# A retention kernel with two feed-forward layers: every load among the retention tiles waits until at most a megabyte of loads is under way ahead of it

## The chip, the cores and the metric

The kernel runs on one core of a Trainium2 chip. The metric is the device time of one execution in microseconds (us); before the change it is 815.48 us, the median of 3 runs (814.66 to 815.95). Names of engines: TensorE (PE in the rows; PEld is its weight load), VectorE (DVE), ScalarE (ACT), GpSimd (POOL) and SyncE (SP), whose queue issues the transfers that are spoken of here.

## What is computed

Retention over 4 batches, 8 heads, 576 positions and 64 channels per head, and then two feed-forward layers without biases on the 2304 tokens of 512 channels:

```python
scores = scale * np.matmul(q, k.transpose(0, 1, 3, 2))
Dmat = np.where(rel >= 0, gamma[:, None, None] ** rel[None, :, :], 0.0)
ret = scores * Dmat[None, :, :, :]
x = np.matmul(ret, v)                       # then (B, H, S, D) -> tokens x 512
h = x @ w_in;  r = np.maximum(h, 0.0);  x = (r * r) @ w_out
h = x @ w_in2; relu6 = np.clip(h + 3.0, 0.0, 6.0); out = (h * relu6 / 6.0) @ w_out2
```

q, k and v are 32-bit floats; the weights are 64-bit floats, which the kernel loads as they are and turns into 32-bit ones on ScalarE and VectorE (`decode`, lines 159 to 196).

## The kernel before

**Retention.** Two batches go together, as a pair, in tiles of 128 positions: four full ones and a last one of 64, so 5 units per pair and 10 in all (`unit`, line 215). A unit makes the scores of a tile (lines 310 and 327 on TensorE; the decay is multiplied in by VectorE in lines 315 and 331), then the products with the values (line 343), the sums of keys times values for the state (line 351) and the product of the earlier state with the queries (line 359). Ahead of line 351 GpSimd scales the keys of the tile (line 292, `scale_keys`). The loop over units puts the scores of unit u ahead of the values of unit u-1 (from unit 3 on).

**Its loads.** For a full unit there are four of 512 KB each: queries and keys for the scores (`load_qk`, line 255, tiles `qkt` or `early`) for either batch, and keys and values (`load_kv`, line 269, tiles `kvt` or `early`) for either batch. The last unit of a pair has one load of queries and keys of 512 KB (line 264) and two transfers of 128 KB for its values (line 279). Between these loads stand weights of the first layer: a load of `w_in` is three transfers, one of 256 KB (line 146) and two of 128 KB (line 148), one of `w_out` is one of 512 KB (line 155); both go to `stage` tiles. The list `order` (lines 19 and following of the launch part, 1019 to 1025) fixes the sequence, 44 loads in all: five weight loads stand at its end, one in front of the second pair's first queries, and one in front of the last unit's.

**What paces them.** All are issued by SyncE's queue, in program order. `load_on` (line 1053) issues what the buffers allow so far. A tile that a buffer's earlier reader still needs makes SyncE wait for that reader. The transfers take turns on eight semaphores, and one that finds its semaphore still in use by the transfer eight places ahead waits for that to land. On top of this stands `behind` (line 1043): before a load it copies one element of an earlier load's tile to a scratch row (`seen`) with a transfer of its own, line 1051. This small transfer has to wait on SyncE's queue until the tile has landed, and the load stands behind it. `landing` lists the loads so far, with the element to be read and a size of 1 for 512 KB and 0.5 for the last unit's values. From the list's end backwards `behind` skips loads until their sizes come to a limit, and reads the one before.

**Behind the retention.** TensorE goes on at once with the first layer, line 454, whose first products need the first weight and the tokens of the first batches only; lines 523, 758 and 938 are its other large groups. Everything behind the retention keeps its order.

Of the kernel before, what the change touches and what calls it, by code (L numbers as in the profile page):

```python
# [76 lines left out]
def retention_moe_moe2(ctx, tc, qk, qk_last, kv, w_in, w_out, w_in2, w_out2, consts, out):  # L77
# [934 lines left out]
    with tc.manual_schedule():  # L1012
# [30 lines left out]
        def behind():  # L1043

            n = len(landing)
            if n >= 8 and n % 2 == 0:
                m, flying = n - 1, 0
                while flying < 4:
                    flying += landing[m][1]
                    m -= 1  # L1050
                nc.sync.dma_start(out=seen[:, n:][:, :1], in_=landing[m][0])

        def load_on(done):

            while order:
                kind, u, k = order[0]
                if release(kind, u, k) > done or kind == "w" and len(order) <= 5 and done < UNITS - 3:
                    return
                order.pop(0)
                behind()  # L1060
                if kind == "w":
                    name = coming[0][1:]
                    load()
                    t = staged[name].bitcast(F32)
                else:
                    t = (load_qk if kind == "qk" else load_kv)(u, k)
                short = kind == "kv" and unit(u)[2] < C
                landing.append((t[:1, 512:513] if kind == "kv" and not short else t[:1, :1], 0.5 if short else 1))
# [234 lines left out]
```

## Time and profile before

| | before |
|---|---|
| median of 3 runs, us | 815.48 (814.66 to 815.95) |
| the profiled execution, us | 817.96 |
| its span, us | 816.2 |
| granted clock, mean over the span | 0.998 |
| TensorE products busy | 806.7 us, 99% |
| weight loads of TensorE busy | 714.7 us, 88% |
| VectorE, ScalarE, GpSimd busy | 617.6, 498.6, 21.6 us |
| first product of line 454 (end of the retention) | 64.64 us |
| DMA moved | 208.67 MB, mean 256 GB/s |

The span counts from the first to the last instruction of the program; the execution's own time is 1.8 us more. Busy time of TensorE is modelled from pipelined products, so a busy TensorE isn't one at its peak. The granted clock is the share of full speed that TensorE was given. The share of the DMA engines is that of 16 engines' time that their packets took; it can pass 1 where packets overlap.

### The profile page before, as it was taken

To read this page: it belongs to the slowest core of one execution; us is meant where nothing else is said; L and a number is where in the kernel's file an instruction comes from. 1 tells how busy PE (TensorE), PEld (TensorE's weight loads), DVE (VectorE), ACT (ScalarE), POOL (GpSimd) and SP (SyncE) were. 2 spreads that over 40 slices of the span, in tenths; PEclk is the share of its full clock that TensorE was granted. 3 is DMA by queue.
4 is the path that set the end of the run, shared out by engine and by line. 5 is a ranking of instruction groups with operands and counts; after the bars stand their busy time and mean duration, and the time that the engine had idled before them with its cause. 6 is when DMAs were issued, how large, how long until landed. Compare 5 with 4: busy or idle time off the path is not lost.

```text
span 816.2 us, 13873 instructions
## 1 busy us (share of the span) xinstructions
PE 806.7 (99%) x5052; PEld 714.7 (88%) x5052; DVE 617.6 (76%) x1121; ACT 498.6 (61%) x918; POOL 21.6 (3%) x25
## 2 busy tenths in 40 slices
PE   9989999999999999999999999999999999999998
PEld 7878888888888888888888999988999888999887
DVE  4878888886988678965996577888477988477765
ACT  2238888777886777777786544665355564444553
POOL 2330000000000000000000000000000000000000
PEclk9999999999999999999999999999999999999999
DMA  9993766655799669975998377589676799676794
GB/s 363 340 318 108 210 194 180 208 181 207 261 335 338 238 202 339 333 260 167 339 319 341 133 250 262 168 276 407 202 248 228 210 317 376 207 257 206 217 347 135
DMA packets 80348, 208.67 MB, mean 256 GB/s; under 512 B 7702, under 2 KB 28822, under 8 KB 80280
## 3 DMA queue, kind: packets, MB, share of 16 engines
q1 hardware_dynamic: 79988, 207.52, 75.0%
q8 instruction: 40, 0.66, 0.3%
q10 hardware_dynamic: 292, 0.27, 0.1%
q14 instruction: 28, 0.23, 0.1%
HBM read 165.29 MB, written 42.47 MB: 255 GB/s over the span
## 4 chain that ended last, share of the span: by engine, by line
PE 91%; DMA 6%; DVE 1%; ACT 1%; issue 1%; SPq 0%; POOL 0%; ACTq 0%
PE hps L454 22%; PE yps L523 21%; PE hps L758 21%; PE yps L938 20%; PE ytail L523 3%; DMA kvt<-in_kv_dram 3%; PE hps L445 2%; DMA early<-in_kv_dram 1%; DMA qkt<-in_qk_dram 1%; DMA wo<-rights 1%; PE vps L343 1%; DMA cst<-in_consts_dram 1%; PE vps L359 0%; PE sps L351 0%; PE aps L327 0%
## 5 line engine op out<-in xcount | busy, mean ns | idle before, releaser
L523 PE MATMUL yps<-g,wo 128*128 128x512 f32 x768 | 184.6, 390 | 0.0
L523 PEld LDWEIGHTS yps<-g,wo 128*128 128x128 f32 x768 | 143.2, 188 | 29.1
L938 PE MATMUL yps<-wo,gop 128*128 128x256 f32 (+1 forms) x804 | 143.5, 336 | 0.5 <-DMA wo<-rights 0.4
L938 PEld LDWEIGHTS yps<-wo,gop 128*128 128x128 f32 x804 | 122.3, 190 | 18.1 <-DMA wo<-rights 1.4
L454 PE MATMUL hps<-xring,win 128*128 128x512 f32 (+1 forms) x576 | 135.7, 381 | 0.0
L454 PEld LDWEIGHTS hps<-xring,win 128*128 128x128 f32 x576 | 105.0, 188 | 20.8
L758 PE MATMUL hps<-xlast,win 128*128 128x384 f32 x576 | 107.9, 335 | 0.0
L758 PEld LDWEIGHTS hps<-xlast,win 128*128 128x128 f32 x576 | 100.4, 188 | 0.9 <-DVE mixed L709 0.9
L491 DVE TENSOR_TENSOR g<-r,g 128x512 fp32r<-128x512 f32 x64 | 44.1, 689 | 51.8 <-ACT g L488 51.6
L758 PE MATMUL hps<-xop,win 128*128 128x384 f32 x432 | 82.2, 334 | 0.0
L758 PEld LDWEIGHTS hps<-xop,win 128*128 128x128 f32 x432 | 75.7, 188 | 0.2
L484 ACT ACTIVATE r<-hps 128x512 f32<-128x512 f32 x68 | 39.4, 579 | 46.5 <-PE hps L454 46.5
L771 ACT ACTIVATE v<-mixed,half_one 128x768 f32<-128x768 f32 x21 | 19.7, 938 | 73.7 <-DVE mixed L709 73.7
L454 PE MATMUL hps<-xown,win 128*128 128x512 f32 x240 | 59.6, 389 | 0.0
L454 PEld LDWEIGHTS hps<-xown,win 128*128 128x128 f32 x240 | 45.0, 188 | 9.4
L200 ACT ACTIVATE gop<-sums 128x512 fp32r<-128x512 f32 x54 | 34.1, 632 | 31.1 <-PE yps L938 27.1
L201 DVE TENSOR_TENSOR gop<-sums,gop 128x512 fp32r<-128x512 f32 x54 | 37.2, 689 | 16.0 <-ACT gop L200 15.8
L487 ACT ACTIVATE r<-r 128x512 f32<-128x512 f32 x80 | 47.0, 588 | 2.1
L201 DVE TENSOR_TENSOR win<-w,win 128x512 fp32r<-128x512 f32 x64 | 44.0, 687 | 4.1 <-ACT win L200 1.8
L175 ACT ACTIVATE a<-stage 128x512 f32<-128x512 f32 x64 | 42.4, 662 | 6.6 <-DMA stage<-in_w_in_dram 6.6
L709 DVE TENSOR_TENSOR xall<-yps,xall 128x256 f32<-128x256 f32 x90 | 37.1, 418 | 11.7 <-ACT xall L905 10.2
L188 DVE SCALAR_TENSOR_TENSOR a<-stage,a 128x512 int32<-128x512 int32 x64 | 44.2, 691 | 2.0
(118 smaller groups left out, 1119.8 us busy)
## 6 DMA issues: line engine op xcount, KB each, us to landing
win<-kept SPq DMA_DIRECT2D x72, 512.0 KB, 5.2
wo<-rights SPq DMA_DIRECT2D x66, 512.0 KB, 4.0
wo<-kept SPq DMA_DIRECT2D x48, 512.0 KB, 6.5
stage<-in_w_out_dram SPq DMA_DIRECT2D x32, 512.0 KB, 4.4
kept<-ready SPq DMA_DIRECT2D x24, 512.0 KB, 6.0
rights<-ready SPq DMA_DIRECT2D x24, 512.0 KB, 3.1
gop<-rights SPq DMA_DIRECT2D x18, 512.0 KB, 6.8
kept<-wo SPq DMA_DIRECT2D x16, 512.0 KB, 5.2
```

The source lines that it names most:

```text
L175: nc.scalar.activation(out=a, in_=high.bitcast(F32), func=ACTF.Abs)
L188: nc.vector.scalar_tensor_tensor(out=a.bitcast(I32), in0=high, scalar=-0x40000000, in1=a.bitcast(I32), op0=ALU.bitwise_and, op1=ALU.bitwis ...
L200: lambda: nc.scalar.activation(out=hi, in_=src, func=ACTF.Copy),
L201: lambda: nc.vector.tensor_tensor(out=lo, in0=src, in1=hi.bitcast(F32), op=ALU.subtract),
L454: nc.tensor.matmul(out=h, lhsT=w[:, wp, kk * 128:kk * 128 + 128], rhs=xs[pos, kk][xp][:, o:o + n], start=m == 0, stop=m == 3 * KD - 1,)
L484: relu.append(lambda r=r, h=hs[k]: nc.scalar.activation(out=r, in_=h, func=ACTF.Relu))
L487: nc.scalar.activation(out=r, in_=r, func=ACTF.Square)
L491: low.append(lambda r=r, hi=hi, lo=lo: nc.vector.tensor_tensor(out=lo, in0=r, in1=hi.bitcast(F32), op=ALU.subtract))
L523: nc.tensor.matmul(out=p, lhsT=w[:, wp, m * 128:m * 128 + 128], rhs=g[pos, c][k][:, gpart, :size], start=c == 0 and e == 0 and not (k and ...
L709: nc.vector.tensor_tensor(out=out_, in0=a, in1=b, op=ALU.add)
L758: nc.tensor.matmul(out=to, lhsT=w[:, wp, o], rhs=x[:, xp, f], start=first and m == 0, stop=last and m == 5, skip_group_check=True,)
L938: nc.tensor.matmul(out=to, lhsT=t[:, gp, rows], rhs=w if part is None else w[:, 256 * part:256 * part + 256], start=name in ("P1", "P5", " ...
```

## The change

`behind` is called ahead of every load, and it reads an element from the ninth load on (n counts the loads so far). Before, it did so only ahead of every second load, and it skipped loads up to a size of 4 (2 MB); now it does so ahead of each, and skips up to a size of 2 (1 MB).

```diff
         def behind():
 
             n = len(landing)
-            if n >= 8 and n % 2 == 0:
+            if n >= 8:
                 m, flying = n - 1, 0
-                while flying < 4:
+                while flying < 2:
                     flying += landing[m][1]
                     m -= 1
                 nc.sync.dma_start(out=seen[:, n:][:, :1], in_=landing[m][0])
```

With n = 8 the loop ended at m = 3 and ends now at m = 5. The number of line 1051's transfers goes from 18 to 36; TensorE's instructions keep their order.

SyncE's queue at the first of these loads, before (qkt and early are queries and keys, kvt and early keys and values; a row is a transfer, x2 two like it in a row):

```order
L275 DMA kvt<-in_kv_dram 128x1024 x2
L1051 DMA seen<-kvt 1x1
L259 DMA qkt<-in_qk_dram 128x1024
L259 DMA early<-in_qk_dram 128x1024
L1051 DMA seen<-qkt 1x1
L259 DMA early<-in_qk_dram 128x1024 x2
L1051 DMA seen<-kvt 1x1
L275 DMA kvt<-in_kv_dram 128x1024
```

The same place now:

```order
L275 DMA kvt<-in_kv_dram 128x1024 x2
L1051 DMA seen<-qkt 1x1
L259 DMA qkt<-in_qk_dram 128x1024
L1051 DMA seen<-kvt 1x1
L259 DMA early<-in_qk_dram 128x1024
L1051 DMA seen<-kvt 1x1
L259 DMA early<-in_qk_dram 128x1024
L1051 DMA seen<-qkt 1x1
L259 DMA early<-in_qk_dram 128x1024
L1051 DMA seen<-early 1x1
L275 DMA kvt<-in_kv_dram 128x1024
```

Each load has a reading transfer of its own ahead of it; the first one reads the sixth load's tile where it read the fourth's.

SyncE's queue at the weight load in front of the last unit, before (stage is the weight):

```order
L275 DMA kvt<-in_kv_dram 128x1024
L146 DMA stage<-in_w_in_dram 128x2x128
L148 DMA stage<-in_w_in_dram 64x2x128 x2
L1051 DMA seen<-qkt 1x1
L264 DMA qkt<-in_qk_last_dram 128x2x512
L275 DMA kvt<-in_kv_dram 128x1024
L1051 DMA seen<-kvt 1x1
L275 DMA kvt<-in_kv_dram 128x1024
L279 DMA kvt<-in_kv_dram 64x512 x2
```

And now:

```order
L275 DMA kvt<-in_kv_dram 128x1024
L1051 DMA seen<-qkt 1x1
L146 DMA stage<-in_w_in_dram 128x2x128
L148 DMA stage<-in_w_in_dram 64x2x128 x2
L1051 DMA seen<-kvt 1x1
L264 DMA qkt<-in_qk_last_dram 128x2x512
L1051 DMA seen<-kvt 1x1
L275 DMA kvt<-in_kv_dram 128x1024
L1051 DMA seen<-stage 1x1
L275 DMA kvt<-in_kv_dram 128x1024
L1051 DMA seen<-qkt 1x1
L279 DMA kvt<-in_kv_dram 64x512 x2
```

A reading transfer stands ahead of the weight load too, and one of those behind it reads the weight's own tile.

## Rows read from the trace of the kernel before

**Rows 1.** Busy time by stretch: length, PE, PEld, DVE, ACT, POOL, granted clock, DMA share, GB/s

```profile
14.10:24.00 9.90, 9.78 (x205) 9.38 (x206) 7.08 (x14) 1.14 (x4) 3.13 (x3) 1.00 1.03 400
24.00:31.00 7.00, 5.86 (x168) 5.41 (x166) 3.85 (x8) 2.69 (x8) 3.06 (x4) 1.00 1.05 307
31.00:41.00 10.00, 9.66 (x201) 8.50 (x193) 9.30 (x17) 1.68 (x5) 2.47 (x2) 1.00 0.98 348
41.00:48.00 7.00, 6.23 (x120) 5.42 (x124) 4.73 (x8) 2.40 (x8) 2.93 (x2) 1.00 1.00 389
48.00:57.00 9.00, 6.68 (x157) 6.14 (x150) 7.29 (x12) 4.88 (x12) 2.16 (x3) 1.00 1.05 295
...
64.60:816.00 751.40, 747.88 (x3920) 662.50 (x3912) 574.76 (x1046) 480.56 (x873) 0.00 (x0) 1.00 0.74 249
```

**Rows 2.** Chain of waits that ended last, 24 to 65 us: start, length, what

```profile
24.11 6.92 DMA qkt<-in_qk_dram
...
37.37 0.57 SPq L1051
...
38.00 6.67 DMA kvt<-in_kv_dram
...
54.67 2.31 issue
```

**Rows 3.** SyncE's instructions in time, 38 to 47 us: start, length, line

```profile
38.00 0.38 SPq L275 DMA_DIRECT2D kvt<-in_kv_dram  x1
38.47 0.89 SPq L259 DMA_DIRECT2D qkt<-in_qk_dram  x1
40.93 0.58 SPq L1051 DMA_DIRECT2D seen<-qkt  x1
...
44.53 0.45 SPq L146 DMA_DIRECT2D stage<-in_w_in_dram  x1
45.02 1.61 SPq L148 DMA_DIRECT2D stage<-in_w_in_dram  x2
46.68 0.64 SPq L1051 DMA_DIRECT2D seen<-qkt  x1
```

**Rows 4.** SyncE's waits, 4 to 24 us: in total, times, longest

```profile
SPq L1051 <- DMA kvt<-in_kv_dram: 3.9, 2, 2.9
SPq L1051 <- DMA early<-in_qk_dram: 2.9, 2, 2.0
```

**Rows 5.** TensorE's products in time, 28 to 66 us; in brackets the idle time before

```profile
29.16 0.98 PE L343 MATMUL vps<-ret,early 128*64 128x128 f32 x13 [1.14 <-issue]
...
50.50 1.09 PE L343 MATMUL vps<-ret,kvt 128*64 128x128 f32 x16
...
56.98 0.57 PE L310 MATMUL aps<-qkt 64*64 64x64 f32 x22 [2.31 <-issue]
57.48 1.61 PE L343 MATMUL vps<-ret,kvt 128*64 128x128 f32 x16
...
59.73 1.82 PE L343 MATMUL vps<-ret,kvt 128*64 128x128 f32 x16
...
64.64 1.67 PE L454 MATMUL hps<-xring,win 128*128 128x512 f32 x6
```

**Rows 6.** Busy time by stretch, around the hole; columns as in rows 1

```profile
47.30:54.30 7.00, 7.00 (x168) 6.60 (x165) 5.24 (x8) 3.56 (x8) 2.09 (x2) 1.00 1.05 318
57.90:61.30 3.40, 3.40 (x46) 3.40 (x42) 2.98 (x6) 0.00 (x0) 2.09 (x4) 0.50 0.87 265
```

**Rows 7.** DMA issues at 513.7 and 749.8 us: count, size, us to landing

```profile
wo<-rights SPq DMA_DIRECT2D x1, 512.0 KB, 3.5
wo<-rights SPq DMA_DIRECT2D x1, 512.0 KB, 3.6
```

**Rows 8.** DMA queues, 19 to 57 us: packets, MB, share of 16 engines

```profile
q8 instruction: 6, 0.10, 1.0%
```

**Rows 9.** GpSimd's instructions in time, 55 to 60 us

```profile
58.48 1.04 POOL L292 TENSOR_TENSOR kvt<-kvt,cst 128x512 f32<-128x512 f32 x1 [0.52 <-DVE ret L315]
```

## The prediction, made before the changed kernel was run

> **What bounds the kernel now.** I read the table of busy time by stretch first [rows 1]. From 64.6 us on TensorE is busy 747.88 of 751.40 us, on instructions that the change doesn't touch. What can move is the retention, the first 64.6 us: if it ends some us later or earlier, so does the kernel, since nothing behind it has slack on TensorE. In the retention TensorE is busy most of the time too, 9.78 of 9.90 us in one stretch, but only 5.86 of 7.00 and 6.68 of 9.00 in two others; and in all of them up to 57 us the DMA engines are loaded to 0.98 to 1.05 of their time.
>
> The chain of waits [rows 2] says which of the two leads. Up to about 45 us it runs through loads (6.92 and 6.67 us from issue to landing stand here) and through the reading transfer of line 1051, which I call a marker. So there the loads set the pace; behind it TensorE is in the chain, with a piece of 2.31 us named issue: TensorE waits for nothing that the profile shows. The SyncE rows [rows 3] show the pattern: a load, a second one, a wait, a marker. SyncE's waits at markers between 4 and 24 us come to 3.9 and 2.9 us for keys, values and queries [rows 4]. Its own time is short, but not by much: a marker holds the queue for 0.57 to 0.64 us and a load for about 0.4 us, 1.0 us together, where half a megabyte takes some 1.3 us to move.
>
> Last, the end of the retention. The 2.31 us stand in front of line 310 [rows 5]; behind them the granted clock is 0.50 (the 1.2 GHz level) over 3.40 us [rows 6], and the same 16 products of line 343 take 1.61 and 1.82 us there, 1.09 us before [rows 5].
>
> **The change, part by part.** Before load n (every one from the ninth on, n counted from 0) SyncE now waits for load n-3, where it waited, on every second one, for load n-5. A load is issued with 1 MB ahead of it, so at most 1.5 MB are under way; before it was 2.5, and 3 with the second load of a pair.
>
> 1. *Eighteen more markers* (36 for 18). 18 by 0.61 us is 11 us of SyncE's time. Only loads stand behind them on that queue. Marker and load together, 1.0 us, stay under the 1.3 us of a load's transfer, so SyncE doesn't become the bound by itself: 0 us. What a marker moves is one element.
>
> 2. *A shorter queue in front of the DMA engines.* The loop is now: load n-3 lands, marker 0.61 us, some 0.1 us of gaps, load n issued and landed. What issue to landing takes with little ahead is shown by two loads of the same 512 KB later in the kernel, 3.5 and 3.6 us [rows 7]; most of the 6.67 and 6.92 us in the retention is queue. So the loop is no shorter than 0.7 + 3.5 = 4.2 us for three loads, 1.40 us each. Before, at 400 GB/s in 14.1 to 24 us [rows 1], a load took 524,288 B / 400 GB/s = 1.31 us. The loss is 0.09 us each. This stretch moved 9.9 us x 400 GB/s = 3.96 MB, 7.6 loads: 0.7 us. In the four later stretches the engines deliver 307, 348, 389 and 295 GB/s, 1.71, 1.51, 1.35 and 1.78 us per load, so the loop of 1.40 us costs only beside the 1.35: 5 loads by 0.05, 0.2 us. Together **+0.9 us**, from 0 (if landing gets shorter with less beside it) to 2 us (if the later stretches are held up too).
>
> The Trainium skill, page "DMA: Bandwidth & Descriptors", section "Anatomy of one DMA", puts a transfer at 2.0 us fixed plus its bytes at 436 GB/s, 3.2 us for this size (a fit for another issue path). By that the loop would be 3.9 us, 1.30 us per load, and this term nothing; the rows have 3.5.
>
> 3. *A load of three transfers.* The weight loads among the retention tiles, two before the last keys, are three transfers each: their issue takes 0.45 and 1.61 us [rows 3] where a tile takes 0.4, so the last third goes out 1.7 us later. With a short window, what is queued ahead has to cover that. Bounds: 0 (covered: 1 MB ahead is 2.6 us) and 2 x 1.7 = 3.4 us. I take **+0.6 us**, near the lower end, since the cover is larger than the gap.
>
> 4. *Instruction fetch on the same engines.* Between 19 and 57 us the DMA queues show 6 instruction packets of q8, 1.0% of 16 engines' time [rows 8]: 0.010 x 16 x 38 / 6 = 1.0 us of one engine each. A load has landed when its last engine is done. With 2.5 MB queued the other fifteen work on while one is late; with 1.5 MB they run dry and wait for it. Bounds: 0 and 6 x 1.0 = 6.0 us. I take **+1.8 us**, 0.3 each: nearer to 0, since the kernel before pays a part already, as its 295 to 389 GB/s against 400 show.
>
> The stream of loads then ends 0.9 + 0.6 + 1.8 = 3.3 us later (0 to 11).
>
> 5. *The end of the retention.* The hole of 2.31 us and the slow clock behind it can go or stay. The clock costs half of 3.40 us, 1.7 us; GpSimd, which scales the last keys, loses 0.52 us in a wait for VectorE that is late through the hole [rows 9]. So at most 2.2 us come back. If tiles come late, TensorE waits there for tiles instead, and the clock may fall all the same: 0. I take the middle, **-1.1 us**, no row being nearer to either.
>
> Sum: 3.3 - 1.1 = **+2.2 us**. The profiled execution took 817.96 us (span 816.2), 2.5 us over the median of 815.48; the change is the same on both: 820.2 for an execution like it, 815.48 + 2.2 = **817.7 us** for the median.
>
> **Rivals.**
> *Faster.* Both holes named issue, 1.14 us in front of line 343 and 2.31 us in front of line 310 [rows 5], fall where instruction packets meet a full queue of loads. If TensorE's next instructions stand behind queued loads, 1.5 MB let them in sooner than 2.5; the hole at 54.7 us and the slow clock go. If three loads also keep the engines busy (terms 2 to 4 at zero), that is 2.2 us faster, 813.3. Against it: over the first hole (28.0 to 29.2 us) the chain runs through a load of 6.92 us from 24.11 [rows 2], so it costs nothing now, and little but the clock is to be had at the second. It decides if the stream slips by under 1 us.
>
> The same page, section "Queues, rings and completion order", says that an engine changes between queues packet by packet, so a deep queue of loads wouldn't hold up a fetch; by that this rival gives 815.5, and counts under the next. No row shows when a fetch was asked for.
>
> *No difference.* The slip stays at 0 to 2 us (with term 4 at nothing, 1.5) and is hidden or given back: from 47.3 to 54.3 us TensorE is busy 7.00 of 7.00 us [rows 6] and leads, so that a slip of 1 us is covered there. 815.5 us.
>
> *Much slower.* Every fetch stops the window once, and nothing comes back at the end: 0.9 + 0.6 + 6.0 = 7.5 us, 823.0. For it: up to 57 us the engines' time is the scarce thing, and what idles there is lost. Against it: the same stretch of 47.3 to 54.3 us, where TensorE paces the loads, and not they it.
>
> *It doesn't do what it says* only in this: behind the last keys, which count half, and behind a weight load, whose marker reads one element of its first third, the window is half a load wider. That is within the bounds.
>
> **How the numbers follow.** About 0.2% (1.6 us) is what a measurement of this kernel can tell from no change. Forecast (+1 to +5 us): 0.45. Faster: 0.21. No difference: 0.22. Much slower: 0.12. At its lower end (+1 to +1.6) the forecast lies within 0.2%, with 0.06 of its 0.45. So faster by over 0.2%: 0.21; within 0.2%: 0.22 + 0.06 = 0.28; slower: 0.39 + 0.12 = 0.51. For 8 in 10 the range runs from 813.2 (the faster rival, nearly whole) to 822.5 (the forecast whole, and the lower part of the much slower rival). The forecast alone: 816.5 to 820.5.
>
> **What would show it.** Right: the rate in 14 to 24 us falls from 400 to some 375 GB/s, tiles land some 4 us after their issue, the DMA engines' share falls under 0.95, and the first product of line 454, at 64.64 us before [rows 5], starts 1 to 5 us later. Term 4: the share falls most behind instruction packets. The faster rival: no wait named issue over 1 us in front of line 310, the granted clock at 1.00 up to line 454, the share still near 1. Wrong altogether: line 454 starts within 1 us of where it did though the share fell, so that TensorE and not the loads set the pace; or the end moves by something behind 64.6 us, where I expect nothing.

## The result, and the profile after

The change makes the kernel slower: 827.96 us, the median of 6 runs (825.15 to 830.85), beside 815.72 us for the kernel before in 6 runs taken with them (814.66 to 816.09). The ratio is 1.0149, with a 95% interval from 1.0124 to 1.0174, so the change costs 12.2 us. The prediction was 817.7 us, in a range that ended at 822.5. The direction was right and the size was not. The profiled execution of the kernel before is one of its slower ones: of the 71 executions of it that were measured beside the experiments, 55 have a mean granted clock of 1.00 and take 815.7 us on the mean, 10 have at most 0.998 and take 818.3 us, and the profiled one has 0.998.

| | before | after |
|---|---|---|
| median, us | 815.72 | 827.96 |
| profiled execution (its span), us | 817.96 (816.2) | 829.04 (827.2) |
| first product of line 454 starts, us | 64.64 | 74.22 |
| from there to the end of the span, us | 751.56 | 752.98 |
| GB/s, 14.1 to 57 us | 349 | 273 |
| DMA engines' share, 14.1 to 57 us | 1.02 | 0.85 |

Of the 11.0 us by which the span grew, 9.6 us lie in the retention. Of the 1.4 us behind it most can be scatter: from line 454's start to the end of the span the profiles of the other kernels of this text take 750.5 to 752.7 us. The table of busy time by stretch of the kernel after has the same columns as [rows 1]: start and end, length, PE, PEld, DVE, ACT, POOL, granted clock, DMA share, GB/s.

```profile
14.10:24.00 9.90, 8.06 (x147) 7.39 (x144) 5.43 (x11) 1.15 (x4) 1.04 (x1) 0.91 0.81 257
24.00:31.00 7.00, 7.00 (x161) 6.43 (x159) 3.90 (x7) 1.14 (x4) 3.13 (x3) 0.89 0.89 308
31.00:41.00 10.00, 6.66 (x113) 5.64 (x112) 4.95 (x11) 2.28 (x6) 2.02 (x3) 0.91 0.92 271
41.00:48.00 7.00, 6.38 (x120) 5.80 (x121) 6.09 (x11) 0.84 (x1) 1.41 (x2) 0.88 0.80 276
48.00:57.00 9.00, 7.23 (x142) 6.13 (x142) 5.06 (x8) 2.12 (x6) 3.16 (x3) 1.00 0.81 264
57.00:64.60 7.60, 6.73 (x156) 5.91 (x145) 5.90 (x8) 2.15 (x6) 2.09 (x2) 1.00 0.93 284
64.60:74.20 9.60, 6.78 (x184) 5.61 (x176) 7.72 (x13) 4.67 (x12) 3.86 (x4) 1.00 0.72 214
74.20:827.00 752.80, 748.08 (x3920) 662.82 (x3912) 574.89 (x1046) 480.92 (x875) 0.00 (x0) 1.00 0.74 250
```

Read the last two columns against [rows 1]. Before, the share of the DMA engines stood at 0.98 to 1.05 in every stretch to 57 us: there was always something queued. Now it is 0.80 to 0.92, all the way. The engines run dry, and not beside single events but throughout. The whole of 14.1 to 57 us in one row, for the kernel before and then for the kernel after:

```profile
14.10:57.00 42.90, 38.22 (x828) 34.86 (x828) 32.24 (x57) 12.79 (x33) 13.75 (x14) 1.00 1.02 349
```

```profile
14.10:57.00 42.90, 35.33 (x670) 31.39 (x670) 25.43 (x44) 7.54 (x21) 10.77 (x11) 0.92 0.85 273
```

At 349 GB/s a load of 524,288 B takes 1.50 us, at 273 GB/s 1.92 us. Before, these 42.9 us moved 42.9 x 349 GB/s = 15.0 MB, 28.6 loads; the same loads take 28.6 x 0.42 = 12 us longer now. The retention's end slipped by 9.6 us.

The chain of waits shows what the loads wait for. These are pieces of it in the kernel after, with start, length and what it is, as in [rows 2]:

```profile
15.25 0.58 SPq L1051
...
15.88 5.94 DMA early<-in_qk_dram
...
21.88 0.58 SPq L1051
...
22.51 3.65 DMA early<-in_kv_dram
...
26.84 5.55 DMA early<-in_kv_dram
...
36.13 4.78 DMA qkt<-in_qk_dram
...
41.59 5.98 DMA kvt<-in_kv_dram
...
48.27 4.34 DMA kvt<-in_kv_dram
...
53.75 4.33 DMA qkt<-in_qk_dram
...
61.37 4.95 DMA qkt<-in_qk_last_dram
```

From 15 to 66 us the chain is mostly the loop of load, marker, load: a load lands, the marker (the reading transfer of line 1051) that waited for it goes out 0.02 to 0.07 us later (once 0.49) and takes 0.58 us, and 0.04 to 0.1 us behind it the next load that the chain runs through is issued. It leaves this loop twice, from 32.4 to 36.1 us and from 58.7 to 61.3 us, where it runs along SyncE's own instructions (markers and the issue of loads, some of two or three transfers). The eight loads take 4.94 us on the mean from issue to landing. Before, the chain left the loads at 45 us and ran through TensorE's work behind that. SyncE's instructions in time, around the first of these steps, in the kernel after:

```profile
16.36 0.59 SPq L1051 DMA_DIRECT2D seen<-qkt  x1
16.99 0.38 SPq L259 DMA_DIRECT2D early<-in_qk_dram  x1
17.91 0.58 SPq L1051 DMA_DIRECT2D seen<-early  x1
18.54 0.39 SPq L275 DMA_DIRECT2D kvt<-in_kv_dram  x1
21.88 0.58 SPq L1051 DMA_DIRECT2D seen<-early  x1
22.51 0.39 SPq L275 DMA_DIRECT2D early<-in_kv_dram  x1
```

Three loads go out within 3 us (at 15.88, 16.99 and 18.54), then SyncE stands from 18.93 to 21.88 us until the first of the three has landed. Compare [rows 3], where a marker stood ahead of every second load. SyncE's waits at markers between 4 and 24 us (total, times, longest), against the 3.9 and 2.9 us of [rows 4]:

```profile
SPq L1051 <- DMA qkt<-in_qk_dram: 5.5, 1, 5.5
SPq L1051 <- DMA early<-in_qk_dram: 3.4, 2, 2.9
```

And TensorE, which waits for tiles now. Its waits between 5 and 75 us in the kernel after:

```profile
PE aps L327 <- DMA qkt<-in_qk_dram: 2.5, 2, 1.4
PE vps L343 <- DMA kvt<-in_kv_dram: 2.5, 4, 0.9
PE aps L327 <- DMA early<-in_qk_dram: 1.8, 1, 1.8
PE aps L310 <- DVE a L179: 1.7, 1, 1.7
```

No row of TensorE's products is named issue; the pieces of 1.14 and 2.31 us of [rows 5] are gone. That brought nothing, since the tiles come later by more. The lower clock level [rows 6] is not gone: it stands elsewhere, in two stretches, each behind a wait of TensorE for a tile of queries and keys (1.84 us in front of 21.95 us, 1.45 us in front of 38.95 us). The granted clock is 1.00 in the rest of the retention, so the 0.88 to 0.91 in the table are means over stretches with a piece of these in them:

```profile
22.20:25.60 3.40, 3.40 (x34) 3.18 (x34) 1.68 (x4) 0.00 (x0) 1.04 (x1) 0.50 0.64 186
39.30:42.60 3.30, 3.30 (x31) 3.07 (x29) 1.84 (x3) 0.00 (x0) 0.00 (x0) 0.50 0.84 272
```

### The profile page after: what moved, and what is told of

It is laid out like the page before. It is cut to its first block, busy times and chain, and to the rows that moved or that the text cites. A ratio compares the mean times of both kernels' runs of the same rounds, so it can differ in the third digit from the quotient of the medians.

```text
span 827.2 us, 13904 instructions
## 1 busy us (share of the span) xinstructions
PE 809.7 (98%) x5052; PEld 715.6 (87%) x5052; DVE 620.2 (75%) x1121; ACT 498.3 (60%) x918; POOL 21.6 (3%) x25
## 4 chain that ended last, share of the span: by engine, by line
PE 86%; DMA 8%; SPq 2%; DVE 1%; ACT 1%; issue 1%; ACTq 0%
PE yps L523 21%; PE hps L454 21%; PE yps L938 20%; PE hps L758 20%; PE ytail L523 3%; DMA kvt<-in_kv_dram 2%; PE hps L445 2%; DMA early<-in_kv_dram 1%; DMA qkt<-in_qk_dram 1%; SPq L1051 1%; DMA wo<-rights 1%; DMA early<-in_qk_dram 1%; DMA stage<-in_w_out_dram 1%; DMA qkt<-in_qk_last_dram 1%; DMA cst<-in_consts_dram 1%
## 5 line engine op out<-in xcount | busy, mean ns | idle before, releaser
L454 PEld LDWEIGHTS hps<-xring,win 128*128 128x128 f32 x576 | 105.2, 188 | 22.2 <-ACT r L484 1.4
```

The costliest lines, as they stand in the source:

```text
L454: nc.tensor.matmul(out=h, lhsT=w[:, wp, kk * 128:kk * 128 + 128], rhs=xs[pos, kk][xp][:, o:o + n], start=m == 0, stop=m == 3 * KD - 1,)
```

## The experiments

All kernels differ from the kernel after by the lines shown, unless the text says that they start from the kernel before. In the code, `flying < 2` is the megabyte: the wait reaches back to the third load ahead; `flying < 4` reaches back to the fifth. That number is called the limit here, and "deeper" means a larger one.

### How deep the window is, and how many markers there are

The change does two things at once: it moves the wait from load n-5 to load n-3, and it puts a marker ahead of every load. The first two kernels are meant to do one each. Every load has a marker, but with the limit of before:

```diff
-                while flying < 2:
+                while flying < 4:
```

> A marker before every load as in the change, but with the old limit: 2 MB ahead. Theory A (depth: with 1 MB ahead the DMA engines run dry whenever one of the sixteen is late, and a load has landed only with the last of them): within 2 us of before, 814 to 818, since the queue is as deep as it was for the first load of a pair. Theory B (SyncE: 18 more markers of 0.6 us each on the queue that issues the loads): the markers are all there, so about as slow as the change, 824 to 829.

Measured: 818.41 us beside 815.85, ratio 1.0024 [1.0011, 1.0038]: some 2 us, a sixth of the change, and just above the range of theory A. But this kernel hasn't the depth of before. A marker is a transfer too and takes a turn of the eight semaphores; with a marker on every load, the transfer eight places ahead of a load is at most the fourth load ahead. SyncE's waits from 14 to 57 us in this kernel (total, times, longest) show that the loads themselves wait, not the markers:

```profile
SPq L275 <- DMA kvt<-in_kv_dram: 2.6, 4, 1.2
SPq L275 <- DMA qkt<-in_qk_dram: 1.4, 1, 1.4
SPq L1051 <- DMA qkt<-in_qk_dram: 1.0, 1, 1.0
```

Counted from the landings, no load of 512 KB goes out here with more than three others under way (1.5 MB); before, it was up to five. So the 2 us can't be put down to the markers' time. Second, every second load alone has a marker, with the new depth:

```diff
-            if n >= 8:
+            if n >= 8 and n % 2 == 0:
```

> The other half alone: a marker before every second load only, as before, with 1 MB ahead instead of 2. Theory A: the second load of a pair goes out with 1.5 MB ahead, so the queue lies between the change and before, and so does the time: 818 to 824. Theory B: no marker more than before, so 815 to 817.

Measured: 824.84 us, 1.0091 [1.0061, 1.0122], just above the range expected. So the depth by itself, at the old number of markers (1 MB ahead of every second load, 1.5 MB ahead of the others), costs 0.0091 x 815.7 = 7.4 us. (Costs in microseconds are worked out from the ratios in this way; the medians, 824.84 and 815.85, would give 9.0.) Between the two depths, with a marker ahead of every load:

```diff
-                while flying < 2:
+                while flying < 3:
```

> A marker before every load with 1.5 MB ahead, between the change (1 MB, +12 us) and e1 (2 MB, +2.6 us). Theory A: with four loads in the loop of 5.6 us a load takes 1.40 us instead of 1.87, close to the 1.31 to 1.5 of before: most of the loss is gone, +3 to +6 us, 819 to 822. A straight line between the two would be +7.3 us, 823.

Measured: 820.38 us beside 816.14, 1.0052 [1.0033, 1.0072]. With a marker on every load the cost goes in steps with the limit, 12.2, 4.2 and 2.0 us for `flying` under 2, 3 and 4; the last two have the same 1.5 MB ahead, once with the marker in the loop and once without it, since there the load itself waits. The rows of 14.1 to 57 us, first a limit of 4 with every load (columns as above), then of 3, then of 2 with every second load:

```profile
14.10:57.00 42.90, 38.58 (x817) 34.51 (x818) 32.43 (x55) 11.53 (x31) 12.61 (x13) 1.00 0.97 330
```

```profile
14.10:57.00 42.90, 38.31 (x806) 34.31 (x810) 30.66 (x53) 9.97 (x27) 12.97 (x13) 1.00 0.94 320
```

```profile
14.10:57.00 42.90, 35.13 (x714) 30.76 (x716) 26.67 (x47) 9.66 (x26) 10.17 (x11) 1.00 0.85 286
```

Share and rate fall together with the depth, and the granted clock is 1.00 in all three, so the third, which runs at 824.84 us, loses without the 0.92 of the kernel after. If the lower clock adds to the loss of the kernel after isn't shown: its six executions have mean clocks of 0.994 to 0.998, and the longest, 830.85 us, has the lowest.

### A marker more, and no marker at all

If the loop of three loads sets the pace, an instruction put into it must show in full, once for every three loads. A second marker behind the first, into a tile of its own:

```diff
+        again = own.tile([1, 64], F32, name="again")
...
                 nc.sync.dma_start(out=seen[:, n:][:, :1], in_=landing[m][0])
+                nc.sync.dma_start(out=again[:, n:][:, :1], in_=landing[m][0])
```

> The change with two markers before each load, the second reading the same element. It doubles the marker's time, 0.6 us, in the loop of load n-3 landed, marker, load n issued and landed, and leaves the depth of the queue. Theory A (the loop's length sets the pace: 0.7 us of SyncE and some 4.9 us from issue to the last engine's landing, in the change's trace): 36 loads by 0.62 us, a third of it each as three are under way, 7.5 us slower than the change, 833 to 838. Theory F (the engines' own slowness with a short queue sets the pace, SyncE's part is covered): within 2 us of the change.

Measured: 834.33 us beside 816.14, 1.0231 [1.0188, 1.0275], which is 6.7 us over the kernel after (6.4 by the medians). 36 markers are 12 rounds of the loop, at some 0.6 us each 7.4 us: nearly all of it shows. It doesn't come in the plain way, though. A load lands after 4.49 us here, 0.6 us sooner than in the kernel after; but from the landing that is waited for to the issue of the load are 1.71 us on the mean, where one marker takes 0.69 us and two would take 1.27. Three loads with two markers each are 4.8 us of SyncE's time in a round of 6.2 us, so they wait for their turn on its queue. SyncE's instructions in that kernel:

```profile
15.37 0.58 SPq L1052 DMA_DIRECT2D seen<-kvt  x1
15.99 0.54 SPq L1053 DMA_DIRECT2D again<-kvt  x1
16.58 0.39 SPq L259 DMA_DIRECT2D early<-in_qk_dram  x1
```

Now the other way: the same wait without any marker. The load itself is made to wait for load n-3, by a dependency between the two instructions:

```diff
-                nc.sync.dma_start(out=seen[:, n:][:, :1], in_=landing[m][0])
+                return issued[m]
...
+                    tc.add_manual_dep(first, upto, mybir.DependencyInfo(
+                        mybir.DependencyClass.Sync, mybir.DependencyReason.DATA), reason="window")
```

> The change's waits without its markers: the load itself waits for load n-3, so 1 MB is ahead as in the change, but the 0.65 us of the marker are gone from the loop. Theory A (loop of marker, issue and landing, 0.7 + 5.1 us for three loads): 36 loads by 0.65 us, a third of it each, is 7.8 us at most, less what landing gains in length as the queue fills: 820 to 824. Theory F (the depth alone sets the pace, SyncE's part is covered): as the change, 826 to 829.

Measured: 823.55 us beside 815.86, 1.0089 [1.0067, 1.0112]. Without a marker the megabyte still costs 7.3 us, so of the 12.2 us some 4.9 are the markers' time in the loop. SyncE in this kernel issues loads alone, and the next row is its stretch of 14.1 to 57 us:

```profile
16.33 0.33 SPq L259 DMA_DIRECT2D early<-in_qk_dram  x1
17.74 0.33 SPq L275 DMA_DIRECT2D kvt<-in_kv_dram  x1
```

```profile
14.10:57.00 42.90, 36.92 (x725) 32.89 (x726) 28.43 (x50) 9.63 (x26) 11.43 (x12) 0.96 0.89 293
```

The same with the limit of before, first on every load and then on every second (the dependency as above). Without markers a load has the eight turns to itself, and in the first of these most loads (15 of 23) do go out with four others under way:

```diff
-                while flying < 2:
+                while flying < 4:
```

> The same with 2 MB ahead of every load. Theory A: the 2.6 us that e1 costs are its markers (5 loads in the loop, 36 by 0.65 / 5 = 4.7 us at most): 815 to 817, like before. Theory F: 818, like e1.

Measured: 816.55 us, 1.0010 [0.9999, 1.0021]. Against the kernel with a marker on every load and the same limit it is 1.1 us less (1.9 by the medians); the two intervals overlap, and half a megabyte more is under way here, so this difference can't be put down to the markers' time either.

```diff
-            if n >= 8:
+            if n >= 8 and n % 2 == 0:
...
-                while flying < 2:
+                while flying < 4:
```

> The waits of the kernel before (every second load, 2 MB ahead) without its 18 markers. Theory A: the deep queue covers the marker's time, so 814.5 to 816.5, within noise of before.

Measured: 816.57 us, 1.0007 [0.9994, 1.0021]: no difference from the kernel before, which is this one with markers. Its line 454 starts at 63.18 us, 1.5 us earlier than before, and its profiled execution is 1.5 us shorter (a span of 814.7 beside 816.2 us): it has no lower clock level in the retention, and the profiled one of before has. The medians show nothing of that.

### No window, and a deeper one

No load waits for another:

```diff
-            if n >= 8:
+            if n >= 99:
```

> No marker at all; what limits the queue is the eight semaphores that the transfers take turns on, up to eight loads. Theory A: not slower than before by its mechanism, 814 to 817; the DMA engines' share stays at 1 up to 57 us. Theory D (fetch of instructions stands behind queued loads: the holes named issue, 1.14 and 2.31 us before, none over 0.2 us in the change): holes longer than before's 2.31 us, and 1 to 4 us slower than before.

Measured: 816.80 us beside 815.85, 1.0000 [0.9986, 1.0013]. The rate is the highest of all; the second fence is TensorE's waits between 5 and 75 us (total, times, longest):

```profile
14.10:57.00 42.90, 37.47 (x824) 34.87 (x825) 33.32 (x56) 12.94 (x33) 13.74 (x14) 1.00 1.04 359
```

```profile
PE aps L310 <- issue: 2.1, 1, 2.1
PE vps L359 <- issue: 1.5, 1, 1.5
PE vps L343 <- issue: 1.5, 1, 1.5
PE aps L327 <- issue: 0.7, 2, 0.3
```

The pieces named issue come to 5.8 us here, 1.14 and 2.31 us before [rows 5], 0.5 us with a marker on every load and a limit of 4, and none after. They do grow with the depth; none is longer than the 2.31 us of before, where theory D expected longer ones and 1 to 4 us of loss. But line 454 starts at 63.36 us in this kernel, and the time is that of before, so they cost little. From the kernel before, with the wait a step deeper on every second load:

```diff
-                while flying < 4:
+                while flying < 5:
```

> The kernel before with 2.5 MB ahead instead of 2. Theory A: before is already deep enough, so 814.5 to 817. Theory D (a deeper queue holds up the instruction packets): the holes named issue stay at 1 to 2.3 us, and it isn't faster than before.

Measured: 815.35 us beside 816.14, 0.9993 [0.9980, 1.0005]. It isn't deeper in fact: here, too, the loads wait for the turn of their semaphore, now for the fifth load ahead, and the loads under way at an issue are 3.4 on the mean, 3.5 before. What shows that more depth brings nothing is the kernel without a limit, with 5.0 under way: from 2 MB on the depth makes no difference that can be measured.

### One engine late

Term 4 of the prediction said that an instruction packet on one DMA engine holds up a short window. These four kernels put eight extra transfers of 16 KB, from memory to memory, ahead of loads of queries and keys. In two they are cut so that all 17 packets go to one engine, in two so that 16 packets are spread over the engines; one pair starts from the kernel after, one from the kernel before. On one engine:

```diff
+                if kind == "qk" and k == 0 and len(landing) >= 8:
+                    extra = dram.tile([17, 120], mybir.dt.int64, tag=f"extra{u}", name="extra")
+                    nc.sync.dma_start(out=extra, in_=w_in2[:17, :120])
```

Spread: the same lines with the shape `[16, 128]` for `[17, 120]`. The expectations stand in the order after on one engine, after spread, before on one engine, before spread:

> The change, with eight more transfers of 16 KB (DRAM to DRAM, 17 rows of 960 bytes, which is meant to go to a single DMA engine), one behind the marker of the first query load of each unit from the third on. Theory A1 (what makes a short queue dear is that a load has landed only with its last engine, so anything that holds one engine up, as an instruction packet of 1 us does, stops the whole window): 5 to 8 us slower than the same kernel with the 16 KB spread over all engines (e6). Theory A2 (it is only the loop's fixed length, marker, issue and landing, whatever a single engine does): within 1.5 us of e6.

> The control of e5: the same eight transfers at the same places, 16 rows of 1 KB, one for each DMA engine. Both theories: the issue of each on SyncE, 0.4 to 0.6 us, lengthens the loop eight times, so 2 to 5 us slower than the change.

> The kernel before with the eight transfers of 16 KB on one engine. Theory A1: the deep queue hides one late engine, so less than 3 us slower than its control e8, clearly less than between e5 and e6. Theory A2: no difference from e8.

> The control of e7: the eight transfers of 16 KB spread over the engines, in the kernel before. Both theories: within 2 us of before, 814 to 818, since SyncE's queue has time there.

Measured, beside 816.09 us:

| eight extra transfers | median, us | ratio [95%] | over the kernel they start from |
|---|---|---|---|
| after, on one engine | 830.90 | 1.0185 [1.0161, 1.0209] | 2.9 |
| after, spread | 832.79 | 1.0212 [1.0190, 1.0234] | 5.1 |
| before, on one engine | 818.33 | 1.0032 [1.0019, 1.0045] | 2.6 |
| before, spread | 819.46 | 1.0040 [1.0019, 1.0060] | 3.3 |

Being on one engine makes nothing worse, in either kernel; the kernel before with the spread transfers was expected within 2 us of before and missed that, and the kernel after on one engine is 1.9 us faster than spread by the medians (their intervals overlap), which neither theory had. What the transfers cost, 2.6 to 5.1 us, is at most about what they take of SyncE's time, 8 x 0.61 = 4.9 us. One of them in the first of the four:

```profile
12.30 0.61 SPq L1063 DMA_DIRECT2D extra<-in_w_in_dram  x1
```

The trace bears out that they go to one engine: the 17 packets start one behind the other, mostly 40 ns apart, where the 16 spread ones overlap. The test has a limit: the 17 packets take some 56 ns each on the mean, 0.95 us on one engine, and if that engine is one that finishes early, they cost nothing there. It speaks against the term and doesn't exclude it for another engine.

### The weights behind the retention

In the kernel after, the products of line 454 are interrupted by a wait that the kernel before doesn't have. TensorE in time:

```profile
74.22 4.45 PE L454 MATMUL hps<-xring,win 128*128 128x512 f32 x24
79.52 9.05 PE L454 MATMUL hps<-xring,win 128*128 128x512 f32 x48 [0.85 <-ACT r L484]
88.41 1.60 PE L523 MATMUL ytail<-gtail,wo 128*128 128x256 f32 x12
```

From 74.22 to 88.41 us are 14.19 us, where the kernel before took 12.68 (64.64 to 77.32). To see if the weight loads' own waits do that, the last five were left without one:

```diff
-                behind()
+                if len(order) >= 5:
+                    behind()
```

> The change, but without markers before the last five loads, the weights behind the retention's tiles. Theory C (part of the loss comes behind the retention, where TensorE waits 0.85 us in front of line 454 for ScalarE and the first layer's opening takes 14.2 us instead of 12.7, because the weights come late): 1 to 2 us faster than the change, 825.5 to 827, with the opening of line 454 back at 12.7 us and the retention's end unchanged at about 74 us. Theories A and B alone: as the change, within its scatter.

```profile
74.14 12.81 PE L454 MATMUL hps<-xring,win 128*128 128x512 f32 x72
86.78 1.60 PE L523 MATMUL ytail<-gtail,wo 128*128 128x256 f32 x12
```

The opening is back at 12.64 us in this kernel's profile. But the time is 827.84 us, 1.0133 [1.0105, 1.0160], the same as the kernel after within both intervals. The 1.5 us are seen in the profiled execution; that they are part of the median isn't shown, and from line 454's start to the end this kernel takes 752.7 us, hardly less than the 753.0 of the kernel after.

## Why the prediction was wrong, step by step

**What bounds the kernel: right.** The table of stretches said that nothing behind 64.6 us has slack, and that in front of it the DMA engines are the scarce thing. Both held: 9.6 of 11.0 us are lost up to line 454, in stretches where the engines' share fell.

**Term 2, the loop of three loads: the step that failed.** The form was right, the size was not. The prediction wrote "what issue to landing takes with little ahead is shown by two loads of the same 512 KB later in the kernel, 3.5 and 3.6 us", and took 0.7 + 3.5 = 4.2 us, 1.40 us per load. Those two loads of [rows 7] had nothing under way when they were issued. The next loads behind them, issued 1.6 us later with one other under way, took 4.28 and 4.67 us in the same trace. In the loop two others are nearly always under way, and the chain of after shows 4.94 us: 0.7 + 4.94 = 5.64 us, 1.88 us per load, 279 GB/s. The measured rate is 273. The prediction's own rows gave both ends, 3.5 us alone and 6.67 to 6.92 us with 2 to 2.5 MB ahead [rows 2], and the text took the lower one as the value, with an upper bound of 2 us for the whole term. The middle of the ends, 5.1 us, would have given (as is easy to say now) 5.8 / 3 = 1.93 us per load, 0.43 over the mean of 1.50 before, and 28.6 x 0.43 = 12 us.

How landing depends on depth can be counted from the trace, at the signals that each of a load's 16 engines gives when its part is done. For retention loads of 512 KB issued between 14 and 57 us, the mean from issue to the first, the middle (eighth) and the last engine, in us:

| kernel | first | middle | last | GB/s |
|---|---|---|---|---|
| the two loads of [rows 7] | 3.00 | 3.23 | 3.53 | |
| after (1 MB, a marker each) | 3.32 | 3.85 | 5.08 | 273 |
| 1 MB, two markers each | 3.07 | 3.44 | 4.49 | 254 |
| 1 MB, no marker | 3.49 | 4.10 | 5.36 | 293 |
| 1.5 MB, a marker each | 3.53 | 4.12 | 5.53 | 320 |
| limit of 4, a marker each (1.5 MB in fact) | 3.65 | 4.34 | 5.62 | 330 |
| before (2 MB, every second) | 4.28 | 4.93 | 6.66 | 349 |
| 2 MB, no marker | 4.67 | 5.14 | 7.37 | 351 |
| no window | 7.48 | 7.83 | 9.72 | 359 |

A wait holds until the last engine is done. Of the 1.55 us by which a load lands later in the window of after than alone, 0.6 us are there at the middle engine already, and 0.9 us lie between the middle and the last: alone the last is 0.3 us behind, here 1.2 us. For a megabyte without markers the loop is 5.36 us for three loads, 1.79 us each, 293 GB/s: what is measured.

**A second fault in the same term.** "In the four later stretches the engines deliver 307, 348, 389 and 295 GB/s ... so the loop of 1.40 us costs only beside the 1.35." With 1.88 us per load the loop is slower than all of the five stretches of [rows 1], 1.31 to 1.78 us, and it can cost in each. The table after shows it: the rate fell in four of them, to 257, 271, 276 and 264 GB/s; in the second, 24 to 31 us, it is 308 where it was 307.

**Term 1, the markers at 0 us: wrong.** "Marker and load together, 1.0 us, stay under the 1.3 us of a load's transfer" says that SyncE's time isn't the bound, and for most of the retention it isn't. But the marker stands between a landing and the next issue, so its time is part of the loop, once for three loads: 36 markers, 12 rounds, 0.7 us with the gaps, 8.4 us, less what the landing is shorter with them (5.08 for 5.36 us, 12 x 0.28 = 3.4 us): 5.0 us. The runs with and without markers at 1 MB differ by 0.0060 in their ratios, 4.9 us. At the old limit a marker ahead of every load costs some 2 us, and there the trace puts it down to the depth: a marker uses up a turn of the eight semaphores.

**Term 3, three-transfer loads, +0.6 us: not settled.** The chain of after has 2.0 us of SyncE's own time in it at the weight load (58.73 to 60.69 us). No run tests the term: the kernel that freed weight loads of their wait freed the last five, not the two among the retention tiles.

**Term 4, instruction fetch, +1.8 us: left open.** The queue of instruction packets is as light as in [rows 8] (packets, MB, share; 14 to 57 us of after):

```profile
q8 instruction: 5, 0.08, 0.8%
```

Of the 21 loads of the table, eleven have such a packet under way in the first 3 us behind their issue: they land after 5.53 us on the mean, with the last engine 1.51 us behind the middle one. The ten others land after 4.59 us, with 0.93 us. The other kernels with a limit of 2 have the same sign (0.2 to 0.6 us), the kernel before hasn't it (6.61 and 6.77 us). So the trace speaks for the direction of the term: with a short window a load beside a fetch lands later. How much of the time that makes isn't shown, and the extra transfers on one engine cost no more than spread ones. It isn't the main part: the ten loads without a packet make a loop of 0.7 + 4.59 us, 1.76 us per load, 0.26 us over the 1.50 of before; all loads together lose 0.42.

**Term 5, the end of the retention, -1.1 us: worth nothing.** The 2.31 us and the lower clock level did go from there: no wait named issue, and this row for the stretch of [rows 6]:

```profile
57.90:61.30 3.40, 2.53 (x46) 2.37 (x46) 3.22 (x6) 1.25 (x2) 0.83 (x1) 1.00 0.93 285
```

TensorE is busy 2.53 of 3.40 us here where it was busy all of it; it waits for tiles instead, as the prediction's other bound had it, and the lower clock level came earlier, behind such waits. That "the change is the same on both", the profiled execution and the median, was wrong here as well: the slow clock belonged to the profiled execution (0.998), and most executions of the kernel before are at 1.00 and had none to give back.

**The rivals.** The faster one was right that the pieces named issue vanish with a shorter queue, and wrong that three loads keep the engines busy: it said that it decides "if the stream slips by under 1 us", and the stream slipped by 9.6. Its first half tells against the rule of the Trainium skill, page "DMA: Bandwidth & Descriptors", section "Queues, rings and completion order", as it was applied there: if the pieces are fetches, which no row shows, and a fetch had its turn whatever the depth, they would not go from 0 over 0.5 and 3.4 to 5.8 us with it. The much slower rival came nearest with 823.0 us, by a mechanism of which the runs show the direction and not the size: that it came near is luck. What spoke against it, that TensorE paces the loads from 47.3 to 54.3 us [rows 6], held for the kernel before only: a loop of its own that is slower than TensorE takes the lead over. The other section of the Trainium skill that was cited, "Anatomy of one DMA" on the same page, gives 3.2 us for a load of this size. The traces here have 3.5 alone and 4.5 to 5.4 in this window, so a sum by it was further off than the one by the row.

**What would show it.** The list named the right rows: the rate in the first stretch (375 GB/s expected, 257 measured), the share under 0.95 (0.85), line 454 later by 1 to 5 us (9.6), tiles some 4 us after their issue (5.08). The first three moved in the direction named, and by more than named; landings are shorter than before's 6.66 us, and by less than named.

## What to carry to other kernels

A window of loads in flight is a loop: landing, the waiter's own issue, the next load's issue. Size it by the landing as it is with the others under way, to the last engine (5.1 us here, where a load alone took 3.5), and put everything that the waiter issues into it; the window has to hold what the wanted rate moves in that time. Count, too, what else bounds the window: here every transfer, the markers included, takes a turn of eight semaphores, and markers on every load left 1.5 MB where 2 were asked for. And a deep queue costs little: from 2 MB ahead to no limit at all the time here didn't change, so in doubt the window is made deeper, or the wait put on the load itself and not on a reading transfer in front of it.

## What the runs showed of the hardware

- The last of a load's 16 engines signals 1.0 to 2.2 us behind the middle one in every window of the table, where it is 0.3 us for the two loads alone. In the kernel after it is 1.51 us for loads with an instruction packet under way in their first 3 us and 0.93 us for the others. Which engine it is, and why, stays open.
- The pieces of TensorE's idle time named issue come with the loads under way at an issue (mean number of 512 KB each): none after (1.9) and with a limit of 3 (2.4), 0.5 us with a limit of 4 and a marker each (2.5), 3.4 us before (3.5), 5.3 us with 2 MB and no markers (3.6), 5.8 us without a limit (5.0). What TensorE fetches in them no row shows.
- A reading transfer of one element takes 0.58 us of SyncE's queue, a load of 512 KB 0.33 to 0.39 us.
- The granted clock fell to 0.50 (the 1.2 GHz level) twice in the profile of after, from 22.2 to 25.6 us and from 39.3 to 42.7 us, each time just behind a wait of TensorE of 1.84 and 1.45 us, and not at all in the retention of the kernel with a marker on every second load and a limit of 2, whose products were as little busy (35.1 us of 42.9, beside 35.3). What sets it stays open.
